# Transposes by DMA or by TensorE in a fused linear-attention and SwiGLU kernel

## The chip, the cores and the metric

The kernel runs on one core of a Trainium2 chip. The metric is the device time of one execution in microseconds (us). TensorE (PE) does the matrix products, VectorE (DVE), ScalarE (ACT) and GpSimd (POOL) the elementwise work, and SyncE (SP) and POOL issue the DMAs.

## The reference, cut to what matters

Eight batches of eight heads, 1024 tokens, head size 64. The keys and values are first projected along the sequence to 64 rows; the attention's output then runs through a gated feed-forward block (FFN) with 512 inputs and 1536 hidden units.

```python
k_proj = np.einsum('ks,bhsd->bhkd', E, k)          # (8, 8, 64, 64)
v_proj = np.einsum('ks,bhsd->bhkd', F, v)
scores = 1.0 / np.sqrt(64) * np.matmul(q, k_proj.transpose(0, 1, 3, 2))
attn = np.exp(scores - np.max(scores, axis=-1, keepdims=True))
attn = attn / (np.sum(attn, axis=-1, keepdims=True) + 1e-09)
x = np.matmul(attn, v_proj)                        # heads side by side: (8192, 512)
g = x @ w_gate
out = (g * (1.0 / (1.0 + np.exp(-g))) * (x @ w_val)) @ w_out
```

## The kernel before

The FFN is the frame. Its main loop has 192 iterations: 16 chunks of 512 tokens (two for each batch) by 12 blocks of 128 hidden units. An iteration has three groups of four matmuls with 512 columns each: `f_g` (gate, L303), `f_v` (value, L318) and, a chunk behind, `f_y` (output, L344). ScalarE takes a tanh of the gate (`th`, L311), VectorE makes the gated product in two instructions (L327, L332), and ScalarE copies the finished output block out of PSUM (`ysb`, L353) for SP to store.

The attention of the next batch is cut into small steps, and each is put by hand into a slot; every iteration has two slots, one after `f_g` and one after `f_y`. All engines run their instructions in the order in which this program writes them. The steps of batch b, for 8 units of work (`u`: 4 heads by 2 of the 8 token groups each):

- `u_KV`: k and v projected, 16 matmuls side by side (`kvp`, L150); v's result is written to the block diagonal of `BDV` (L164, L165).
- `u_KT`: the projected k transposed and put on the block diagonal of `BD` (L174, L182).
- `u_T`: four 128x128 transposes of q on TensorE into PSUM (`qTp`, L195) and a copy `qT` out of it. For batches 2 to 7 (`BY_DMA`) `u_TD` does this for half a batch with one DMA transpose from SP (`qTd`, L207).
- `u_S`: four score matmuls (`sc`, L229) and the exponential `ee` on ScalarE; `u_R`: sum and reciprocal on VectorE (`zz`, `rr`); `u_N`: the product on POOL (L260), which gives `AA`, or `AAd` for batches 2 to 7.
- `u_A`: four transposes of `AA` on TensorE (`aTp`, L276) and a copy `AT`. For batches 2 to 7 `u_AD` does this for half a batch with one DMA transpose from SP (L214).
- `u_PV`: one matmul for a pair of heads (`pv`, L287) and a copy into `xT`, the FFN's input.

`place(b)` gives the slots: a batch has 48 of them, and `s0 = 48 * (b - 1)` is where its projection stands. The loads of k, v and q (with a conversion to bf16) are issued from POOL, in POOL's order among its products. PSUM buffers for all attention steps in the loop come from one pool of three (`ps_a`).

Batch 0's first half comes ahead of the loop, in an order written out. k comes in four quarters by SP in float32 (`kraw`) and is converted head by head (`cast_k`), seven by VectorE and POOL and the last by ScalarE; POOL issues its loads of q, v and weights after its own conversion. `warm(n)` are n dummy matmuls whose results nothing reads.

Of the kernel before, what the change touches and what calls it, by code (L numbers as in the profile page):

```python
# [15 lines left out]
B = 8  # L16
H = 8
# [10 lines left out]
CH = 2  # L28
CW = 512
NIT = B * CH * NFT  # L30
BY_DMA = range(2, B)


@with_exitstack
def kernel(
# [22 lines left out]
    const = ctx.enter_context(tc.tile_pool(name="const", bufs=1))  # L58
    w_pool = ctx.enter_context(tc.tile_pool(name="weights", bufs=1))
    kv_pool = ctx.enter_context(tc.tile_pool(name="kv", bufs=2))  # L60
    q_pool = ctx.enter_context(tc.tile_pool(name="qbf", bufs=4))
    aw = ctx.enter_context(tc.tile_pool(name="aw", bufs=2))
    x_pool = ctx.enter_context(tc.tile_pool(name="xT", bufs=2))
# [76 lines left out]
    def u_KV(b, what="kv", hs=(0, H), at="a"):  # L140

        key = (b, what)
        if key not in kvp:
            kvp[key] = bank(at, [P, H, D], FP32, "kvp")
        t = kvp[key]
        h0, h1 = hs
        todo = [x for x in (("k", 0, ET, kb), ("v", 64, FT, vb)) if x[0] in what]
        for j in range(NJ):
            for _, lo, w, src in todo:
                nc.tensor.matmul(  # L150
                    out=t[lo : lo + 64, h0:h1].rearrange("p h d -> p (h d)"),
                    lhsT=w[:, j, :],
                    rhs=src[b][:, h0:h1, j, :],
                    start=(j == 0),
                    stop=(j == NJ - 1),
                )
        if "k" in what:
            if (b, "s") not in kvp:
                kvp[b, "s"] = aw.tile([KP, H, D], BF16, name="ks", tag="ks")
            nc.scalar.copy(out=kvp[b, "s"][:, h0:h1], in_=t[0:64, h0:h1])  # L160
        if "v" in what:
            tv = t[64:128].rearrange("p (a c) d -> p a c d", c=2)
            ps = slice(h0 // 2, h1 // 2)
            nc.vector.tensor_copy(out=BDV[b % 2][0:64, ps, 0:64], in_=tv[:, ps, 0, :])  # L164
            nc.vector.tensor_copy(out=BDV[b % 2][64:128, ps, 64:128], in_=tv[:, ps, 1, :])  # L165
        if h1 == H:
            kvp.pop(key)

# [32 lines left out]
        copy(eng, t[:], ps[:])  # L201
        qT[b, u] = t

    def u_TD(b, ch):

        t = aw.tile([P, 2 * H, P], BF16, name="qTd", tag="qTd")
        nc.sync.dma_start_transpose(  # L207
            out=t[:], in_=qb[b, ch][:].rearrange("p h j d -> p (h j d)")
        )
        qT[b, ch, "d"] = t  # L210

    def u_AD(b, ch):
        t = aw.tile([P, 4, NPAIR, P], BF16, name="AT", tag="AT")
        nc.sync.dma_start_transpose(  # L214
            out=t[:].rearrange("p j a t -> p (j a) t"),
            in_=AA.pop((b, ch, "d"))[:].rearrange("p j h k -> p (j h k)"),
        )
        AT[b, ch] = t

    def u_S(b, u, at="a"):  # L220
        ch, w = divmod(u, 4)
        g, i = divmod(w, 2)
        ps = bank(at, [P, 4, P], FP32, "sc")
        if b in BY_DMA:
            t = qT[b, ch, "d"][:].rearrange("p (h i) t -> p i h t", i=2)[:, i, 4 * g : 4 * g + 4]
        else:
            t = qT.pop((b, u))
        for n in range(4):
            nc.tensor.matmul(  # L229
                out=ps[:, n, :], lhsT=t[:, n, :], rhs=BD[b % 2][:, 4 * g + n, :], start=True, stop=True  # L230
            )
        e = aw.tile([P, 4, 2, KP], FP32, name="ee", tag="ee", bufs=4)
        nc.scalar.activation(  # L233
            out=e[:].rearrange("p h j k -> p (h j k)"),
            in_=ps[:].rearrange("p a k -> p (a k)"),
            func=AF.Exp,
            scale=scale,
        )
        ee[b, u] = e
# [7 lines left out]
        rr[b, u] = r  # L247

    def u_N(b, u):
        ch, w = divmod(u, 4)  # L250
        g, i = divmod(w, 2)
        if b in BY_DMA:
            if (b, ch, "d") not in AA:
                AA[b, ch, "d"] = aw.tile([P, 4, H, KP], BF16, name="AAd", tag="AAd")
            a = AA[b, ch, "d"][:, 2 * i : 2 * i + 2, 4 * g : 4 * g + 4, :]
        else:
            a = AA[b, u] = aw.tile([P, 2, 4, KP], BF16, name="AA", tag="AA", bufs=4)
            a = a[:]
        eng = nc.vector if b == 0 and u == 3 else nc.gpsimd
        eng.tensor_tensor(  # L260
            out=a.rearrange("p j h k -> p h j k"),
            in0=ee.pop((b, u))[:],
            in1=rr.pop((b, u))[:].unsqueeze(3).to_broadcast([P, 4, 2, KP]),
            op=ALU.mult,
        )

    def u_A(b, u, eng=nc.vector):
        ch, w = divmod(u, 4)
        g, i = divmod(w, 2)
        if (b, ch) not in AT:  # L270
            AT[b, ch] = aw.tile([P, 4, NPAIR, P], BF16, name="AT", tag="AT")
        ps = ps_a.tile([P, 2, 2, P], BF16, name="aTp", tag="pa")
        a = AA.pop((b, u))
        for pr in range(2):
            for j in range(2):
                nc.tensor.transpose(  # L276
                    out=ps[:, j, pr, :],
                    in_=a[:, j, 2 * pr : 2 * pr + 2, :].rearrange("p h k -> p (h k)"),
                    identity=ident_bf[:],
                )  # L280
        copy(eng, AT[b, ch][:, 2 * i : 2 * i + 2, 2 * g : 2 * g + 2, :], ps[:])

    def u_PV(b, ch, pr, eng=nc.scalar):
        if (b, ch) not in xT:
            xT[b, ch] = x_pool.tile([P, NPAIR, CW], BF16, name="xT", tag=f"xT{ch}")
        ps = ps_a.tile([P, CW], FP32, name="pv", tag="pa")
        nc.tensor.matmul(  # L287
            out=ps[:].rearrange("p (j t) -> p j t", t=P),
            lhsT=BDV[b % 2][:, pr, :],
            rhs=AT[b, ch][:, :, pr, :],  # L290
            start=True,
            stop=True,
        )
        copy(eng, xT[b, ch][:, pr, :], ps[:])
# [71 lines left out]
    def place(b):  # L366
        s0 = 48 * (b - 1)
        if b == 1:
            put(34, u_KV, 1, "k")
            put(36, u_KT, 1)  # L370
            put(41, u_KV, 1, "v")
            tt = (36, 37, 38, 39, 48, 50, 52, 54)
            sa = (37, 38, 39, 40, 49, 51, 53, 55)
            ta = (42, 43, 44, 45, 54, 56, 58, 60)
            sp = (45, 46, 46, 47, 62, 63, 64, 65)
        else:
            put(s0, u_KV, b)
            put(s0 + 3, u_KT, b)
            o = 14 if b == 2 else 6
            put(s0 + (3 if b == 2 else -6), u_TD, b, 0)  # L380
            put(s0 + (5 if b == 2 else -4), u_TD, b, 1)
            sa = [s0 + o + 3 * j for j in range(NJ)]
            put(sa[3] + 4, u_AD, b, 0)
            put(sa[7] + 4, u_AD, b, 1)
            sp = [s0 + i for i in (39, 41, 43, 45, 57, 59, 61, 63)]
        for j in range(NJ):
            if b not in BY_DMA:
                put(tt[j], u_T, b, j)
                put(ta[j], u_A, b, j)
            put(sa[j], u_S, b, j)  # L390
            put(sa[j] + 1, u_R, b, j)
            put(sa[j] + 1, u_N, b, j)
        for i in range(8):
            put(sp[i], u_PV, b, i // 4, i % 4)

# [4 lines left out]
    with tc.manual_schedule():  # L400
        ef = []
        for which, src in (("E", E), ("F", F)):
            raw = const.tile([KP, S], FP32, name=f"{which}raw")
            ef.append(raw)
        nc.sync.dma_start(out=ef[0][:], in_=E)
        kraw = [
            aw.tile([P, 2, NJ * D], FP32, name="kraw", tag=tag) for tag in ("qTd", "qTd", "AAd", "AAd")
        ]
        for i in range(4):
            nc.sync.dma_start(  # L410
                out=kraw[i][:],
                in_=k[0, 2 * i : 2 * i + 2].rearrange("h (p j) d -> p h (j d)", j=NJ),
            )
        nc.sync.dma_start(out=ef[1][:], in_=F)
# [6 lines left out]
        new_k(0)  # L421

        def cast_k(eng, h):
            copy(eng, kb[0][:, h].rearrange("p j d -> p (j d)"), kraw[h // 2][:, h % 2])

        def turn(which):
            for half in range(2):
# [21 lines left out]
        turn(0)  # L449
        warm(4)  # L450
        for h in range(7):
            cast_k(nc.gpsimd if h == 3 else nc.vector, h)
        load_q(0, 0, 2)
        load_v(0, 2)
        load_w_gv(0)
# [12 lines left out]
        u_S(0, 1, "g")  # L468
        u_S(0, 2, "a")
        u_S(0, 3, "a")  # L470
        for u in range(3):
            u_R(0, u)
            u_N(0, u)
        u_KV(0, "v", (0, 4), at="y")
        u_R(0, 3)
        u_N(0, 3)
        u_A(0, 0, nc.scalar)
        warm(2)
        u_A(0, 1, nc.scalar)
        u_KV(0, "v", (4, 8), at="y")  # L480
        u_A(0, 2, nc.scalar)
        u_PV(0, 0, 0, nc.vector)
        u_PV(0, 0, 1, nc.vector)
        u_A(0, 3, nc.scalar)
        u_PV(0, 0, 2, nc.scalar)
        u_PV(0, 0, 3, nc.vector)
        load_w_gv(2)
# [21 lines left out]
        for b in range(1, B):  # L509
            place(b)  # L510
        for b in range(2, B):
            s0 = 48 * (b - 1) - (12 if b == 2 else 24)
            put(s0, load_k, b)
            put(s0 + 2, load_v, b)
            put(s0 + 4, load_q, b, 0)
            put(s0 + 6, load_q, b, 1)

        for s in slots:
            slots[s].sort(key=lambda x: x[0] not in (load_k, load_v, load_q))
# [48 lines left out]
```

## Time and profile before

| | us |
|---|---|
| median of 3 runs (582.72 to 582.86) | 582.82 |
| the profiled execution | 582.86 |
| its span, first to last instruction | 581.1 |
| TensorE busy | 567.6 (98%) |
| VectorE busy | 337.7 (58%) |
| ScalarE busy | 242.4 (42%) |
| POOL busy | 106.8 (18%) |

The span is what the profile shows from the first instruction to the last; the profiled execution's own time has 1.8 us more around it. Busy times are sums of instruction lengths in which overlaps on an engine count once. A row of the timeline gives the start, the length, the engine, the line, the operation with its output and inputs, and in brackets how long the engine had been idle and what ended that. Matmuls are pipelined, so the pace of TensorE is read from one start to the next and not from a matmul's length.

### The profile page before, as it was taken

The numbers are of one execution on the slowest core, as the hardware profiler recorded it, in microseconds if no ns is written. First come the engines' busy times: TensorE is split into PE (matmuls) and PEld (weight loads), VectorE is DVE, ScalarE is ACT, GpSimd is POOL, SyncE is SP. The second block draws the span as 40 slices with busy tenths as digits, with TensorE's granted clock in tenths as the row PEclk, the third lists the DMA queues.
The fourth block names the chain that finished last, engine by engine and source line by source line (L and its number), as shares of the span: only waits on it lengthen the run. The fifth ranks groups of instructions, "written<-read, shape, count | busy, mean of one in ns | idle before, by whom it ended". The sixth has DMA issues, their size and how long they took to land.

```text
span 581.1 us, 7901 instructions
## 1 busy us (share of the span) xinstructions
PE 567.6 (98%) x2952; PEld 268.1 (46%) x2952; DVE 337.7 (58%) x576; ACT 242.4 (42%) x428; POOL 106.8 (18%) x119
## 2 busy tenths in 40 slices
PE   5999999999999999999999999999999999999997
PEld 3644444544444444444444444444444444444443
DVE  2787564766556664666546764566555674545550
ACT  2545435454435434354345434354343533443321
POOL 5625040224102320025001240022300220000000
PEclk9999999999999999999999999999999999999999
DMA  9999955309930399016980289313990124001012
GB/s 223 190 200 192 205 87 100 73 19 170 203 81 37 80 194 179 37 45 110 177 159 29 63 145 197 74 38 77 183 193 37 38 55 73 37 36 37 19 37 91
DMA packets 100599, 61.34 MB, mean 106 GB/s; under 512 B 51792, under 2 KB 91216, under 8 KB 100560
## 3 DMA queue, kind: packets, MB, share of 16 engines
q0 software_dynamic: 40176, 28.84, 34.3%
q1 hardware_dynamic: 60384, 31.99, 23.9%
q8 instruction: 23, 0.38, 0.3%
q14 instruction: 16, 0.13, 0.1%
HBM read 60.29 MB, written 16.78 MB: 133 GB/s over the span
## 4 chain that ended last, share of the span: by engine, by line
PE 94%; ACT 2%; DVE 2%; DMA 1%; issue 0%; SPq 0%; DVEq 0%; ACTq 0%
PE yps L344 28%; PE vps L318 28%; PE gps L303 28%; PE kvp L150 3%; PE sc L229 3%; PE pv L287 2%; DMA kraw<-in_k_dram 1%; DVE hT L332 1%; PE qTp L195 1%; PE aTp L276 1%; ACT qT L138 0%; DVE s L327 0%; DVE zz L244 0%; PE kTp L174 0%; ACT ysb L353 0%
## 5 line engine op out<-in xcount | busy, mean ns | idle before, releaser
L327 DVE SCALAR_TENSOR_TENSOR s<-th,gps 128x512 f32<-128x512 f32 x192 | 130.5, 680 | 136.1 <-ACT th L311 135.8
L303 PE MATMUL gps<-xT,wg 128*128 128x512 bf16 x768 | 197.9, 379 | 0.5 <-ACT xT L138 0.3
L318 PE MATMUL vps<-xT,wv 128*128 128x512 bf16 x768 | 197.2, 379 | 0.0
L344 PE MATMUL yps<-wo,hT 128*128 128x512 bf16 x768 | 194.6, 379 | 0.7 <-ACT ysb L353 0.7
L311 ACT ACTIVATE th<-gps 128x512 f32<-128x512 f32 x192 | 114.7, 597 | 154.4 <-PE gps L303 152.7
L332 DVE TENSOR_TENSOR hT<-s,vps 128x512 bf16<-128x512 f32 x192 | 132.0, 688 | 22.8 <-PE vps L318 2.5
L344 PEld LDWEIGHTS <-hT 128*128 128x128 bf16 x768 | 75.1, 98 | 91.5 <-issue 1.0
L318 PEld LDWEIGHTS <-wv 128*128 128x128 bf16 x768 | 72.9, 98 | 83.4 <-issue 4.0
L303 PEld LDWEIGHTS <-wg 128*128 128x128 bf16 x768 | 73.1, 98 | 81.9 <-issue 1.0
L260 POOL TENSOR_TENSOR AAd<-ee,rr 128x512 bf16<-128x512 f32 x48 | 49.9, 1040 | 300.6 <-issue 165.3
L353 ACT ACTIVATE ysb<-yps 128x512 f32<-128x512 f32 x64 | 38.2, 597 | 76.0 <-PE yps L344 76.0
L138 ACT CAST xT<-pv 128x512 bf16<-128x512 f32 x61 | 35.4, 584 | 50.4 <-PE pv L287 50.4
L244 DVE TENSOR_REDUCE zz<-ee 128x8 f32<-128x512 f32 x64 | 43.5, 680 | 20.0 <-ACT ee L233 19.7
L233 ACT ACTIVATE ee<-sc 128x512 f32<-128x512 f32 x64 | 38.0, 597 | 20.0 <-PE sc L229 18.8
L260 POOL TENSOR_TENSOR AA<-ee,rr 128x512 bf16<-128x512 f32 x15 | 15.5, 1040 | 63.7 <-DVE rr L246 25.8
L287 PE MATMUL pv<-AT,BDV 128*128 128x512 bf16 x64 | 23.6, 379 | 0.9 <-ACT AT L138 0.7
L229 PEld LDWEIGHTS <-qTd 128*128 128x128 bf16 x192 | 14.8, 98 | 11.3
L150 PE MATMUL kvp<-kb,ET 128*64 128x512 bf16 (+1 forms) x72 | 17.1, 389 | 1.7 <-POOL kb L138 1.0
L229 PE MATMUL sc<-BD,qTd 128*128 128x128 bf16 x192 | 18.6, 219 | 0.0
L246 DVE RECIPROCAL rr<-zz 128x8 f32<-128x8 f32 x64 | 13.0, 203 | 6.3
L164 DVE CAST BDV<-kvp 64x256 bf16<-64x256 f32 (+1 forms) x9 | 3.6, 396 | 22.3 <-ACT ks L160 20.0
L150 PE MATMUL kvp<-vb,FT 128*64 128x512 bf16 (+1 forms) x72 | 16.4, 375 | 0.0
(50 smaller groups left out, 157.1 us busy)
## 6 DMA issues: line engine op xcount, KB each, us to landing
out_dram<-ysb SPq DMA_DIRECT2D x64, 256.0 KB, 2.3
qb<-in_q_dram POOLq DMA_DIRECT2D x15, 512.0 KB, 17.2
kb<-in_k_dram POOLq DMA_DIRECT2D x7, 1024.0 KB, 11.5
vb<-in_v_dram POOLq DMA_DIRECT2D x7, 1024.0 KB, 14.0
kraw<-in_k_dram SPq DMA_DIRECT2D x4, 512.0 KB, 6.0
wg<-in_moe_w_gate_dram POOLq DMA_DIRECT2D x6, 256.0 KB, 10.2
wv<-in_moe_w_val_dram POOLq DMA_DIRECT2D x6, 256.0 KB, 10.7
wo<-in_moe_w_out_dram POOLq DMA_DIRECT2D x2, 768.0 KB, 15.4
```

The lines of the kernel that those rows point to most:

```text
L150: nc.tensor.matmul(out=t[lo : lo + 64, h0:h1].rearrange("p h d -> p (h d)"), lhsT=w[:, j, :], rhs=src[b][:, h0:h1, j, :], start=(j == 0), ...
L229: nc.tensor.matmul(out=ps[:, n, :], lhsT=t[:, n, :], rhs=BD[b % 2][:, 4 * g + n, :], start=True, stop=True)
L233: nc.scalar.activation(out=e[:].rearrange("p h j k -> p (h j k)"), in_=ps[:].rearrange("p a k -> p (a k)"), func=AF.Exp, scale=scale,)
L244: nc.vector.reduce_sum(out=z[:], in_=e[:], axis=AX.X)
L260: eng.tensor_tensor(out=a.rearrange("p j h k -> p h j k"), in0=ee.pop((b, u))[:], in1=rr.pop((b, u))[:].unsqueeze(3).to_broadcast([P, 4, 2 ...
L303: nc.tensor.matmul(out=ps[:], lhsT=wg[:, kt, f * P : (f + 1) * P], rhs=x[:, kt, :], start=(kt == 0), stop=(kt == NKT - 1),)
L311: nc.scalar.activation(out=th[:], in_=ps[:], func=AF.Tanh, scale=0.5)
L318: nc.tensor.matmul(out=ps[:], lhsT=wv[:, kt, f * P : (f + 1) * P], rhs=x[:, kt, :], start=(kt == 0), stop=(kt == NKT - 1),)
L327: nc.vector.scalar_tensor_tensor(out=s1[:], in0=th[:], scalar=1.0, in1=g[:], op0=ALU.add, op1=ALU.mult)
L332: nc.vector.tensor_tensor(out=hT[c][:, f, :], in0=s1[:], in1=ps[:], op=ALU.mult)
L344: nc.tensor.matmul(out=yy[c][:], lhsT=hT[c][:, f, i * P : (i + 1) * P], rhs=wo[:, f, :], start=(f == 0), stop=(f == NFT - 1),)
L353: nc.scalar.activation(out=ysb[:], in_=yy.pop(c)[:], func=AF.Copy, scale=0.5)
```

## The change

Batches 2 to 7 lose the DMA transposes: `u_TD`, `u_AD` and `BY_DMA` go, and all batches use `u_T` and `u_A`. `AT` is laid out with the pair of heads ahead of the token group, so that `u_PV` reads contiguous columns. The slots of batches 2 to 7 are new, and so are the slots of their loads. `kraw` gets a pool of its own in place of the buffers of `qTd` and `AAd`. In batch 0, POOL converts head 1 (in the first quarter of k) in place of head 3; ScalarE copies v's block diagonals; the sums and products of all four units stand ahead of v's projection, and the second half of v is projected after the fourth unit's transposes; some copies change between ScalarE and VectorE.

```diff
-BY_DMA = range(2, B)
...
+    raw_pool = ctx.enter_context(tc.tile_pool(name="raw", bufs=1))
...
-            nc.vector.tensor_copy(out=BDV[b % 2][0:64, ps, 0:64], in_=tv[:, ps, 0, :])
-            nc.vector.tensor_copy(out=BDV[b % 2][64:128, ps, 64:128], in_=tv[:, ps, 1, :])
+            eng = nc.vector if b else nc.scalar
+            copy(eng, BDV[b % 2][0:64, ps, 0:64], tv[:, ps, 0, :])
+            copy(eng, BDV[b % 2][64:128, ps, 64:128], tv[:, ps, 1, :])
...
-    def u_TD(b, ch):
-    def u_AD(b, ch):
...
-            AT[b, ch] = aw.tile([P, 4, NPAIR, P], BF16, name="AT", tag="AT")
+            AT[b, ch] = aw.tile([P, NPAIR, 4, P], BF16, name="AT", tag="AT")
...
-            rhs=AT[b, ch][:, :, pr, :],
+            rhs=AT[b, ch][:, pr].rearrange("p j t -> p (j t)"),
...
             put(s0, u_KV, b)
             put(s0 + 3, u_KT, b)
-            o = 14 if b == 2 else 6
-            put(s0 + (3 if b == 2 else -6), u_TD, b, 0)
-            put(s0 + (5 if b == 2 else -4), u_TD, b, 1)
-            sa = [s0 + o + 3 * j for j in range(NJ)]
-            put(sa[3] + 4, u_AD, b, 0)
-            put(sa[7] + 4, u_AD, b, 1)
-            sp = [s0 + i for i in (39, 41, 43, 45, 57, 59, 61, 63)]
+            tt = [s0 + 8 + 5 * j for j in range(NJ)]
+            sa = [t + 2 for t in tt]
+            ta = [t + 7 for t in tt]
+            sp = [s0 + i for i in (36, 39, 41, 44, 57, 59, 62, 64)]
         for j in range(NJ):
-            if b not in BY_DMA:
-                put(tt[j], u_T, b, j)
-                put(ta[j], u_A, b, j)
+            put(tt[j], u_T, b, j)
             put(sa[j], u_S, b, j)
             put(sa[j] + 1, u_R, b, j)
             put(sa[j] + 1, u_N, b, j)
+            put(ta[j], u_A, b, j)
...
-            cast_k(nc.gpsimd if h == 3 else nc.vector, h)
+            cast_k(nc.gpsimd if h == 1 else nc.vector, h)
...
-        for u in range(3):
+        for u in range(4):
             u_R(0, u)
             u_N(0, u)
+        warm(2)
+        u_A(0, 0, nc.scalar)
         u_KV(0, "v", (0, 4), at="y")
-        u_R(0, 3)
-        u_N(0, 3)
-        u_A(0, 0, nc.scalar)
-        warm(2)
         u_A(0, 1, nc.scalar)
+        u_A(0, 2, nc.scalar)
+        u_PV(0, 0, 0, nc.scalar)
+        u_PV(0, 0, 1, nc.vector)
+        u_A(0, 3, nc.vector)
         u_KV(0, "v", (4, 8), at="y")
-        u_A(0, 2, nc.scalar)
-        u_PV(0, 0, 0, nc.vector)
-        u_PV(0, 0, 1, nc.vector)
-        u_A(0, 3, nc.scalar)
         u_PV(0, 0, 2, nc.scalar)
         u_PV(0, 0, 3, nc.vector)
...
-            s0 = 48 * (b - 1) - (12 if b == 2 else 24)
-            put(s0, load_k, b)
-            put(s0 + 2, load_v, b)
-            put(s0 + 4, load_q, b, 0)
-            put(s0 + 6, load_q, b, 1)
+            s0 = 48 * (b - 2)
+            put(s0 + 36, load_k, b)
+            put(s0 + 40, load_v, b)
+            put(s0 + 36, load_q, b, 0)
+            put(s0 + 44, load_q, b, 1)
```

More of the change, by code (lines that the diff above doesn't have):

```diff
@@ L202, in u_T @@
         qT[b, u] = t
-    def u_TD(b, ch):
[L206 to L210, printed above, removed]
-    def u_AD(b, ch):
[L213 to L218, printed above, removed]
     def u_S(b, u, at="a"):
-        ch, w = divmod(u, 4)
-        g, i = divmod(w, 2)
+        g = (u % 4) // 2
         ps = bank(at, [P, 4, P], FP32, "sc")
[L224 to L227, printed above, removed]
+        t = qT.pop((b, u))
         for n in range(4):
@@ L249, in u_N @@
     def u_N(b, u):
[L250 to L258, printed above, removed]
+        a = aw.tile([P, 2, 4, KP], BF16, name="AA", tag="AA", bufs=4)
         eng = nc.vector if b == 0 and u == 3 else nc.gpsimd
         eng.tensor_tensor(
-            out=a.rearrange("p j h k -> p h j k"),
+            out=a[:].rearrange("p j h k -> p h j k"),
             in0=ee.pop((b, u))[:],
@@ L265, in u_N @@
         )
+        AA[b, u] = a
     def u_A(b, u, eng=nc.vector):
@@ L276, in u_A @@
                 nc.tensor.transpose(
-                    out=ps[:, j, pr, :],
+                    out=ps[:, pr, j, :],
                     in_=a[:, j, 2 * pr : 2 * pr + 2, :].rearrange("p h k -> p (h k)"),
@@ L280, in u_A @@
                 )
-        copy(eng, AT[b, ch][:, 2 * i : 2 * i + 2, 2 * g : 2 * g + 2, :], ps[:])
+        copy(eng, AT[b, ch][:, 2 * g : 2 * g + 2, 2 * i : 2 * i + 2, :], ps[:])
     def u_PV(b, ch, pr, eng=nc.scalar):
@@ L287, in u_PV @@
         nc.tensor.matmul(
-            out=ps[:].rearrange("p (j t) -> p j t", t=P),
+            out=ps[:],
             lhsT=BDV[b % 2][:, pr, :],
-            rhs=AT[b, ch][:, :, pr, :],
+            rhs=AT[b, ch][:, pr].rearrange("p j t -> p (j t)"),
             start=True,
@@ L405 @@
         nc.sync.dma_start(out=ef[0][:], in_=E)
-        kraw = [
-            aw.tile([P, 2, NJ * D], FP32, name="kraw", tag=tag) for tag in ("qTd", "qTd", "AAd", "AAd")
-        ]
+        kraw = raw_pool.tile([P, H, NJ * D], FP32, name="kraw")
         for i in range(4):
             nc.sync.dma_start(
-                out=kraw[i][:],
+                out=kraw[:, 2 * i : 2 * i + 2],
                 in_=k[0, 2 * i : 2 * i + 2].rearrange("h (p j) d -> p h (j d)", j=NJ),
@@ L423, in cast_k @@
         def cast_k(eng, h):
-            copy(eng, kb[0][:, h].rearrange("p j d -> p (j d)"), kraw[h // 2][:, h % 2])
+            copy(eng, kb[0][:, h].rearrange("p j d -> p (j d)"), kraw[:, h])
         def turn(which):
```

## Prediction

> **What bounds the kernel now.** I read the page first, then TensorE's list of waits, then the windows, and last the timeline around the operations that the change moves. The page's span, busy times and chain of waits:
>
> ```profile
> span 581.1 us, 7901 instructions
> PE 567.6 (98%) x2952; PEld 268.1 (46%) x2952; DVE 337.7 (58%) x576; ACT 242.4 (42%) x428; POOL 106.8 (18%) x119
> PE 94%; ACT 2%; DVE 2%; DMA 1%; issue 0%; SPq 0%; DVEq 0%; ACTq 0%
> ```
>
> TensorE is busy for 98% of the span and holds 94% of the chain; VectorE and ScalarE are about half idle. A busy TensorE need not be one at its peak, so I ask what it waits for. All its waits of the whole run, with total, times, longest (us):
>
> ```profile
> PE efp L431 <- DMA Eraw<-in_E_dram: 4.6, 1, 4.6
> PE kvp L150 <- POOL kb L138: 1.0, 1, 1.0
> PE kvp L150 <- ACT kb L138: 0.7, 1, 0.7
> PE yps L344 <- ACT ysb L353: 0.7, 1, 0.7
> PE pv L287 <- ACT AT L138: 0.7, 1, 0.7
> ```
>
> The longest are all in the first 26 us, but for the 0.7 us on ysb, which is in the tail. The same list for 120 to 565 us alone is empty. Two answers show that this middle is also dense: one stretch of the windows, and the chain's pieces for the k and v projections of batches 3 and 4 (start, length).
>
> ```profile
> 300.00:365.00 65.00, 65.00 (x336) 30.41 (x336) 39.18 (x66) 27.62 (x49) 11.87 (x12) 1.00 0.61 107
> ```
>
> ```profile
> 164.18 1.85 PE kvp L150 x16
> ...
> 232.13 1.85 PE kvp L150 x16
> ```
>
> One batch period is 232.13 - 164.18 = 67.95 us. It holds 24 FFN iterations of three groups of four 512-column matmuls; a group takes 0.864 us from its start to the next start in the timeline, so 72 x 0.864 = 62.2. With the projections (1.85), eight groups of scores (8 x 0.22), eight PV matmuls (8 x 0.215) and the four small transposes of k (0.22), that is 67.75. So 0.2 us of the period is slack: there is no gap into which TensorE work could be put for nothing.
>
> **Part 1, the transposes of batches 2 to 7.** Removed: 24 DMA transposes on SP's queue (12 of q, 12 of the normalised scores). Added for each of 6 batches and 8 units: four 128x128 transposes of q and a copy qT on ScalarE, four 128x128 transposes of AA and a copy AT on VectorE. Counting the two instruction lists gives 6 x 8 x 2 = 96 groups of four on TensorE, 384 transposes, each with its weight load; 48 more qT copies on ScalarE and 48 more AT copies on VectorE. All other counts in the middle stay.
>
> What does a group cost? Batches 0 and 1 do exactly this already, so the trace has the row (start, length, then what; the next start is what counts, since lengths overlap):
>
> ```profile
> 84.48 0.39 PE L276 MATMUL aTp<-ident_bf,AA 128*128 128x128 bf16 x4
> 84.71 1.03 PE L303 MATMUL gps<-xT,wg 128*128 128x512 bf16 x4
> 85.57 0.39 PE L276 MATMUL aTp<-ident_bf,AA 128*128 128x128 bf16 x4
> 85.80 1.03 PE L318 MATMUL vps<-xT,wv 128*128 128x512 bf16 x4
> ```
>
> 84.71 - 84.48 = 0.23 us for four, and the group behind it again takes its usual 0.86 (84.71 to 85.57). The groups at 81.67 and 98.37 give 0.22 and 0.23. A second bound comes from a period that holds such work: from batch 2's projections (93.77) to batch 3's (164.18) is 70.41, 2.46 more than the later periods, for eight transpose groups and four score groups more: 0.205 each. So 0.205 to 0.23; I take 0.22, the nearest to most rows: 96 x 0.22 = **+21.1 us** (19.7 to 22.1), all on the path, because TensorE has no idle time there. As a share of the middle: 3.5 us on each of six periods.
>
> The Trainium skill ("TensorE: Matmul & The Clock Gate", Part 4) speaks against this edit more strongly: about 275 ns for a transpose in a kernel, and transposes that do not count as activity for the clock gate. By that figure the sum would be 384 x 0.275 = 106 us; the 84.48 row has about 57 ns for each, and the stretch from 70 to 160 us, which holds such groups, a granted clock of 1.00, so I use the rows. The same page's sustained spacing for 128 columns with weight loads (section "Back-to-back issue gap", 81 ns) would make it 31 us; no row after 30 us shows that pace.
>
> The copies: 48 x 0.58 = 28 us on ScalarE (L138 qT, 580 ns) and 48 x 0.42 = 20 us on VectorE (AT, 424 ns). They are hidden: in the 65 us stretch above ScalarE has 37 us free and VectorE 26, and a period adds 4.6 and 3.4 us. What would uncover them is a short distance. For batch 0 the scores come one slot after the transpose and wait: the group at 38.60 (q) is followed by vps at 38.83, and the scores start at 39.93 instead of 39.69, 0.24 late. The new slots put scores two slots after q's transpose (about 2.9 us) and AA's transpose four slots after the normalisation; on average a copy has twice the room. I put this at 0, with 48 x 0.24 = 11.5 us if the cover is gone (rival 3).
>
> Removing the DMA transposes frees SP's queue, where outputs stand behind them, and DMA time. Nothing on TensorE waits for either from 120 to 565 us, so the gain is 0. PV's moving operand becomes contiguous: a pv matmul in the strided form is already spaced 0.21 us (87.75 to 87.96), the pace of any 512 columns, so 0.
>
> The loads of batch b move later: k and the first q to 12 slots ahead of the projection (24 before), v to 8. By POOL's order, which runs a DMA issue when the normalisation before it has ended, v is issued behind the normalisation of slot 12 ahead. Twelve slots are six iterations of 3 x 0.864 and about 2.1 us of small groups, 17.6; that normalisation ends some 2.8 us into them (116.7 to 119.8 from scores to normalisation, less a slot's 1.3, plus its 1.04): 14.8 us are left. In the trace v lands 13.2 to 14.9 us after issue, with q and transposes beside it; with the transposes gone and k issued 7 us rather than 3.6 us earlier I expect under 12. So 0, with rival 2 if not.
>
> **Part 2, the start.** The first FFN matmul is at 25.36 us and the last copy that its first group needs ends at 26.25. The rows (start, length, engine):
>
> ```profile
> 7.66 0.86 POOL L138 CAST kb<-kraw 128x512 bf16<-128x512 f32 x1 [5.84 <-DMA kraw<-in_k_dram]
> 8.47 1.79 POOL L110 DMA_DIRECT2D qb<-in_q_dram  x2
> ...
> 11.47 0.62 ACT L138 CAST kb<-kraw 128x512 bf16<-128x512 f32 x1 [0.63 <-DMA kraw<-in_k_dram]
> ...
> 24.93 0.59 PE L287 MATMUL pv<-AT,BDV 128*128 128x512 bf16 x2 [0.67 <-ACT AT L138]
> ...
> 25.56 0.69 DVE L138 CAST xT<-pv 128x512 bf16<-128x512 f32 x1 [0.56 <-PE pv L287]
> ```
>
> (a) POOL now casts head 1, which lands with the first quarter at 5.70, so q's load is issued at 5.70 + 0.86 = 6.56 instead of 8.47, 1.9 us earlier; v's and the first weights' issues follow it. But q is not late today: its transposes follow kTp without a wait. And k is still moving: its quarters land at 5.70, 7.63, 8.98 and 11.47, and the last, which shares the engines with q from about 9 us, took 2.5 us instead of 1.4 to 1.9. The earlier q shares with two quarters. TensorE's second half of k waits for that landing. So no gain, and 0 to +1.9; I take +0.6, nearer to the 0.6 to 1.1 us that today's sharing costs one quarter.
>
> (b) The new order for batch 0: all four reduces go ahead of v's projection, two dummy matmuls fill in, then AA's transposes, with v's second half behind the fourth. The third unit's reduce no longer stands behind v's diagonals on VectorE (VectorE waited 0.29 us there, normalisation 3 ended at 23.16). ScalarE in exchange gets four diagonal copies (about 0.3 us each by VectorE's 0.29 for 64x128) in its queue, and PV of pairs 2 and 3 now waits for v's second half and its copies. Re-timing the rows: AA 0 is ready at 20.2 in both; v's first half ends at 21.6 at full pace or 22.5 at the pace of 18.93 (1.92 us for eight); ScalarE then has two diagonals (0.6), AT 1, AT 2 and xT 0 (0.58 each) in line; AA 3's transpose follows, v's second half, two more diagonals, PV, and the last xT at 26.8 or 27.7 against 26.25: +0.6 to +1.5. From below, the two waits of TensorE just ahead of the first FFN group (0.24 and 0.67) are all that can be saved: -0.9. I take +0.4.
>
> Behind this the FFN runs on as before, so the start adds **+1.0 us** (-0.9 to +3.4). The warm clock is the unsure piece: 512-column matmuls run at 0.46 us until 7.5 and at 0.22 from 21, though the granted clock reads 1.00.
>
> **Sum.** The profiled execution took 582.86 us, its span 581.1 and 1.8 around it; the median is 582.82, the same within 0.04. 582.86 + 21.1 + 1.0 = **605.0 us**. Its own range: 582.9 + 19.7 - 0.9 = 601.7 to 582.9 + 22.1 + 3.4 = 608.4.
>
> **Rivals.** 1, not slower: the transposes slip beneath the long matmuls, as TensorE's busy time is modelled. It decides if a group costs under 0.012 us (1.2 us, 0.2%, over 96), giving 582 to 584; the rows above have 0.22 for every group, so 2%. 2, v comes late: if a landing takes 16 us instead of under 14.8, each of five projections (batches 3 to 7) waits 1.2 us or more, +6 and up: 611 to 616. Against it, less traffic beside it; 6%. 3, the scores wait for the qT copies as in batch 0: +11.5, 616; against it, the double distance; 5%. 4, TensorE stays at half pace longer in the start, because it now waits for AA 0 and does less before: each us at half pace loses 0.5, +3 to +5 beyond my value: 608 to 610; 9%.
>
> **How the numbers follow.** My forecast has 78%. The range 602.3 to 608.5 takes nearly all of it and part of rival 4; rivals 1 to 3 are left out, with a little of the low end. About 0.2%, 1.2 us, is what a measurement of this kernel can tell from no change: faster 0.01, same 0.01 (both rival 1), slower 0.98.
>
> **What would show it.** Right: periods of batches 3 to 7 of 71.3 to 71.6 us instead of 67.95, 256 transposes each of q and AA at 0.22 us for four, still no waits of TensorE in the middle, the first FFN group up to 2 us later. Wrong: a period under 70 (a group is cheaper), waits of kvp on a landing (rival 2), of sc on qT (rival 3), or half-pace matmuls past 23 us (rival 4).

## The result, and the profile after

| | before | changed |
|---|---|---|
| median (4 runs each) | 582.84 us | 605.09 us |
| lowest to highest | 582.72 to 583.03 | 603.61 to 606.30 |
| ratio to before, 95% interval | | 1.038 (1.0354 to 1.0406) |
| profiled execution, its span | 582.86, 581.1 | 604.41, 602.6 |

The forecast was 605.0 us, in a range from 602.3 to 608.5. The page of the changed kernel, with the same lines as before:

```profile
span 602.6 us, 8703 instructions
...
PE 587.3 (97%) x3336; PEld 287.4 (48%) x3336; DVE 356.5 (59%) x620; ACT 266.8 (44%) x480; POOL 106.9 (18%) x119
...
PE 93%; ACT 2%; DVE 2%; DMA 1%; issue 0%; SPq 0%; POOL 0%; DVEq 0%; ACTq 0%
```

TensorE has 384 instructions more (3336 - 2952), which are the 384 transposes, and 19.7 us more busy time. It holds the chain as it did. VectorE's 18.8 and ScalarE's 24.4 us of added copies leave both far from full. TensorE's waits between 120 and 590 us, with total, times and longest, are one line:

```profile
PE yps L318 <- ACT ysb L327: 0.7, 1, 0.7
```

It is the same 0.7 us of the tail as before. So no new wait came into the middle, and the added time there is work. The chain's pieces for the projections of batches 3 and 4:

```profile
167.33 1.85 PE kvp L150 x16
...
238.86 1.85 PE kvp L150 x16
```

A period is 238.86 - 167.33 = 71.53 us, against 67.95: 3.58 more, inside the 71.3 to 71.6 that was forecast. TensorE's timeline shows why (start, length):

```profile
197.78 0.39 PE L250 MATMUL aTp<-ident_bf,AA 128*128 128x128 bf16 x4
198.00 0.39 PE L210 MATMUL sc<-BD,qT 128*128 128x128 bf16 x4
198.22 1.03 PE L292 MATMUL vps<-xT,wv 128*128 128x512 bf16 x4
```

Four transposes take 0.22 us from their start to the next start, exactly as the four score matmuls behind them.

The profile also splits the whole run. Before, batch 2's projections start at 93.77 us and 487.3 us remain to the end of the span; in the changed kernel they start at 93.57 and 509.0 remain. The middle and tail therefore cost 21.7 us. The start came out 0.2 us earlier in this one execution, but the runs of one kernel now spread by 2.7 us, so the start needs more than one profile.

### The profile page after: what moved, and what is told of

Read it like the earlier page. It is cut to its first block, busy times and chain, and to the rows that moved or that the text cites. A ratio compares the mean times of both kernels' runs of the same rounds, so it can differ in the third digit from the quotient of the medians.

```text
span 602.6 us, 8703 instructions
## 1 busy us (share of the span) xinstructions
PE 587.3 (97%) x3336; PEld 287.4 (48%) x3336; DVE 356.5 (59%) x620; ACT 266.8 (44%) x480; POOL 106.9 (18%) x119
## 4 chain that ended last, share of the span: by engine, by line
PE 93%; ACT 2%; DVE 2%; DMA 1%; issue 0%; SPq 0%; POOL 0%; DVEq 0%; ACTq 0%
PE yps L318 27%; PE vps L292 27%; PE gps L277 27%; PE kvp L150 3%; PE sc L210 2%; PE pv L261 2%; PE aTp L250 2%; PE qTp L196 2%; DMA kraw<-in_k_dram 1%; DVE hT L306 1%; ACT ee L214 0%; ACT qT L138 0%; DVE s L301 0%; DVE zz L225 0%; ACT ysb L327 0%
## 5 line engine op out<-in xcount | busy, mean ns | idle before, releaser
L233 POOL TENSOR_TENSOR AA<-ee,rr 128x512 bf16<-128x512 f32 x63 | 65.5, 1041 | 411.7 <-DVE rr L227 271.8
L327 ACT ACTIVATE ysb<-yps 128x512 f32<-128x512 f32 x64 | 38.2, 597 | 71.3 <-PE yps L318 71.3
L138 ACT COPY qT<-qTp 128x512 bf16<-128x512 bf16 x62 | 36.0, 582 | 24.8 <-PE qTp L196 24.8
L138 DVE COPY AT<-aTp 128x512 bf16<-128x512 bf16 x61 | 25.7, 422 | 22.4 <-PE aTp L250 21.7
L250 PEld LDWEIGHTS <-AA 128*128 128x128 bf16 x256 | 19.3, 98 | 17.5 <-POOL AA L233 3.1
L250 PE MATMUL aTp<-ident_bf,AA 128*128 128x128 bf16 x256 | 24.8, 219 | 1.9 <-POOL AA L233 1.6
L210 PE MATMUL sc<-BD,qT 128*128 128x128 bf16 x256 | 24.8, 219 | 1.4 <-ACT qT L138 0.6
L196 PEld LDWEIGHTS <-qb 128*128 128x128 bf16 x256 | 19.0, 98 | 12.6 <-issue 0.6
L196 PE MATMUL qTp<-ident_bf,qb 128*128 128x128 bf16 x256 | 24.4, 219 | 0.0
```

What stands on the lines that cost most here:

```text
L138: (nc.scalar.copy if eng is nc.scalar else eng.tensor_copy)(out=out, in_=in_)
L196: nc.tensor.transpose(out=ps[:, n, :], in_=src[:, 4 * g + n, 2 * i : 2 * i + 2, :].rearrange("p j d -> p (j d)"), identity=ident_bf[:],)
L233: eng.tensor_tensor(out=a[:].rearrange("p j h k -> p h j k"), in0=ee.pop((b, u))[:], in1=rr.pop((b, u))[:].unsqueeze(3).to_broadcast([P, 4 ...
L250: nc.tensor.transpose(out=ps[:, pr, j, :], in_=a[:, j, 2 * pr : 2 * pr + 2, :].rearrange("p h k -> p (h k)"), identity=ident_bf[:],)
L327: nc.scalar.activation(out=ysb[:], in_=yy.pop(c)[:], func=AF.Copy, scale=0.5)
```

## The experiments

Theory A: the change costs TensorE's time for 96 groups of transposes, and the rest is small. The rivals were that waits, copies or the DMA transposes hold a part, or the start. Times are compared with the kernel before in the same series of runs, where its median lay between 581.6 and 582.2 us.

### The new start alone

The kernel before, with the changed kernel's start.

```diff
-            cast_k(nc.gpsimd if h == 3 else nc.vector, h)
+            cast_k(nc.gpsimd if h == 1 else nc.vector, h)
...
+            eng = nc.vector if b else nc.scalar
+            copy(eng, BDV[b % 2][0:64, ps, 0:64], tv[:, ps, 0, :])
+            copy(eng, BDV[b % 2][64:128, ps, 64:128], tv[:, ps, 1, :])
...
+        for u in range(4):
+            u_R(0, u)
+            u_N(0, u)
+        warm(2)
...
```

> The kernel before with the new start alone (POOL converts head 1, ScalarE copies batch 0's diagonals, new order of batch 0); the DMA transposes and all slots stay. Theory A (the transposes carry all the cost, the start saves a little): the profile of the changed kernel has its first FFN group at 24.75 us instead of 25.36, so 582.2, within 0.6 us of the kernel before. Theory B (the start costs what was forecast): 583.3 to 584.5. Second question, the spread of the changed kernel (603.6 to 606.3 over four runs, against 582.7 to 583.0): if it comes from the start, these runs spread by 2 us or more; if from the middle, by under 0.5 us.

It took 583.48 us against 581.97, a ratio of 1.0024 (1.0012 to 1.0036): 1.4 us slower (0.7 to 2.1). Theory A had the sign of the start wrong, having read it from one profile. The spread could not be told apart by this series: both kernels spread by over 2 us (12 runs 582.2 to 584.9, 17 runs of before 581.0 to 583.9), so it is not the change's own.

The profile places 0.8 to 1.1 of the 1.4 us. From the start of the scores of batch 0's units 1 to 3 to the first FFN group it takes 25.36 - 17.10 = 8.26 us in the new order. The kernel before has 25.36 - 17.51 = 7.85, with its scores at half pace, and the two kernels with the old order under "The new middle alone" and "Term (a) alone" have 7.63 and 7.58: 0.4 to 0.7 us. The first FFN group to batch 2's projections takes 68.82 us against 68.41, 0.41 more, through one wait that all profiles of the new order have and none of the old one. TensorE's timeline of this kernel:

```profile
17.10 1.00 PE L230 MATMUL sc<-BD,qT 128*128 128x128 bf16 x12
...
24.91 0.61 PE L288 MATMUL pv<-AT,BDV 128*128 128x512 bf16 x2 [0.63 <-ACT BDV L138]
25.36 1.32 PE L304 MATMUL gps<-xT,wg 128*128 128x512 bf16 x4
...
49.69 0.40 PE L277 MATMUL aTp<-ident_bf,AA 128*128 128x128 bf16 x4 [0.37 <-POOL AA L261]
```

The same stretch of the kernel before:

```profile
17.51 1.49 PE L229 MATMUL sc<-BD,qT 128*128 128x128 bf16 x12
...
25.36 1.32 PE L303 MATMUL gps<-xT,wg 128*128 128x512 bf16 x4
```

The first wait is that of PV on ScalarE's copies of v's second half to the diagonal. Before, the same matmuls waited 0.67 us on AT: one wait has been replaced by another of nearly the same length, and the path to it is longer. The second wait is on POOL's product for the last unit of batch 0. That product is late, and so is all of VectorE's work from the reciprocal of the second unit in the loop on, which starts at 44.88 us instead of 44.46; what that reciprocal waits for was not found.

### The new middle alone

The changed kernel with the old start.

```diff
-            cast_k(nc.gpsimd if h == 1 else nc.vector, h)
+            cast_k(nc.gpsimd if h == 3 else nc.vector, h)
...
-            eng = nc.vector if b else nc.scalar
...
-        for u in range(4):
+        for u in range(3):
             u_R(0, u)
             u_N(0, u)
...
```

> The changed kernel with the old start (POOL converts head 3, VectorE copies the diagonals, old order of batch 0); the transposes of batches 2 to 7 on TensorE, the new slots and loads stay. Theory A: 96 groups of 0.224 us = 21.5 us on 582.8, 604.3, periods of 71.53 us, first FFN group back at 25.4. Theory B (part of the cost is the start's): 602.5 to 603.8. The spread: if it comes from the new start, these runs stay within 0.5 us; if from the middle, they spread by 2 us.

603.93 us, ratio 1.0373 (1.0353 to 1.0394): 21.7 us on 582.0. From batch 2's projections (93.09) to the end of the span (602.2) are 509.1 us, as in the changed kernel, and 21.8 more than before: 0.226 to 0.227 a group. Theory A holds for the middle.

### q's load let go by the second quarter again

```diff
-            cast_k(nc.gpsimd if h == 1 else nc.vector, h)
+            cast_k(nc.gpsimd if h == 3 else nc.vector, h)
```

This is in the changed kernel.

> The changed kernel, with POOL converting head 3 again, so that q's first load is let go after k's second quarter. The forecast's term (a) had the earlier release cost 0 to 1.9 us through k's landing: then k's last quarter lands earlier here than the 10.85 us of the changed kernel, and the time is 0.6 us lower, 604.5. The rival (release is free or helps, since k landed at 10.85 there against 11.47 in the kernel before): k's last quarter lands at 11.4 to 11.5, TensorE's second half of k starts 0.6 us later, and the time is 0.3 to 0.6 us higher, 605.5.

605.21 us, ratio 1.0398 (1.0379 to 1.0418), which overlaps the changed kernel's interval. k's last quarter was converted from 12.1 us on, later than in the changed kernel (10.85) or the kernel before (11.47), against the forecast's term (a), but a landing of one execution proves little. From the scores to the first FFN group it took 8.31 us, though TensorE ran the scores at half pace (the row of twelve score matmuls is 1.49 us long, against 1.01 in the changed kernel).

### Term (a) alone

The kernel before with head 1 on POOL, and nothing else.

> The kernel before with one edit: POOL converts head 1, so q's first load is let go by k's first quarter; batch 0's order stays. With the whole new start the kernel before was 1.4 us slower (ratio 1.0012 to 1.0036). If term (a) of the forecast (the earlier q load delays k) is behind that: +0.6 to +1.4 us. If it is the new order (b): no change, within 0.5 us.

581.67 us, ratio 0.9999 (0.9987 to 1.0011). The earlier release of q does nothing that shows, so term (a) is 0 within 0.8 us, and the start's 1.4 us belongs to the order and the diagonals.

### The transposes of q twice

In batches 2 to 7 of the changed kernel each transpose of q is issued twice into the same place.

```diff
-        for n in range(4):
+        for n in [n for n in range(4) for _ in range(2 if b > 1 else 1)]:
             nc.tensor.transpose(
```

> The changed kernel with every transpose of q in batches 2 to 7 issued twice into the same PSUM place: 48 more groups of four on TensorE, with no further copy, DMA or wait. Theory A (the cost of the change is TensorE's own time, 0.224 us a group): 48 x 0.224 = 10.8 us more than the changed kernel, about 616, period 71.53 + 1.79 = 73.3 us. Theory B (a good part of the 21.6 us is for copies, waits and distances that come with a transpose): clearly less, under 6 us.

614.06 us, ratio 1.0559 (1.0536 to 1.0583), 0.0179 above the changed kernel's: 10.4 us. The pieces of its chain:

```profile
241.61 1.85 PE kvp L150 x16
...
314.92 1.85 PE kvp L150 x16
```

The period is 73.31, 1.78 us more for 8 groups, 0.223 each. These transposes came with no copy, wait or DMA, so a group's price is TensorE's own time. It comes to 56 ns for a transpose from one start to the next, where the Trainium skill ("TensorE: Matmul & The Clock Gate", Part 4) has about 275 ns in a kernel; the measurement decides. The page's figure is one transpose's duration, which is 219 ns in the changed kernel's rows; what the time pays for is the spacing.

### The DMA transposes put back, idle

The changed kernel with 24 DMA transposes of q from SP whose results nothing reads.

```diff
+    def u_XD(b, ch):
+        t = aw.tile([P, 2 * H, P], BF16, name="xd", tag="xd", bufs=1)
+        nc.sync.dma_start_transpose(
+            out=t[:], in_=qb[b, ch][:].rearrange("p h j d -> p (h j d)")
+        )
...
+            for i, d in enumerate((4, 18, 32, 40)):
+                put(s0 + d, u_XD, b, i % 2)
```

> The changed kernel with 24 DMA transposes of q issued again from SP in batches 2 to 7, into a buffer that nothing reads (as many as the change removed, between the stores of the output). Theory A (nothing on TensorE's path waits for them, so taking them away gained nothing): 605, within 1 us of the changed kernel, periods of 71.53 us. Theory B (their removal gained time, which the added transposes hid in the sum): slower by 1 us or more, periods above 71.6.

609.72 us, ratio 1.0473 (1.0449 to 1.0498): (1.0473 - 1.038) x 582 = 5.4 us above the changed kernel, which I had not expected. The list of waits names the cause:

```profile
PE kvp L150 <- DMA vb<-in_v_dram: 2.5, 3, 1.1
```

For batches 3 to 7 v's load took 15.8 to 17.1 us to land instead of 12.3 to 13.3, and the new slots leave 167.26 - 151.59 = 15.7 us between its issue and its use. This is the forecast's rival 2, which the changed kernel misses by 2.4 us. The list's 2.5 us count only the time in which TensorE had nothing running. From the FFN group ahead of the projections to the one behind them these five batches take 3.8 us more than in the changed kernel, which covers all of this profile's longer middle (512.6 us against 509.0); its start was 1.1 us later as well. Does anything else cost? The same kernel with the loads of batches 3 to 7 twelve slots earlier:

```diff
+            e = 0 if b == 2 else 12
-            put(s0 + 36, load_k, b)
+            put(s0 + 36 - e, load_k, b)
...
```

> The kernel with 24 idle DMA transposes, with the loads of k, v and q for batches 3 to 7 put 12 slots earlier. Theory A (the idle transposes cost time only by making v land late: v took 15.8 to 17.1 us, and 15.7 us are left between its issue and its use): with 12 slots more there is no wait of kvp on vb, periods are 71.53 us, 604 to 605.5. Theory B (the transposes cost time in another way as well, on TensorE or on the stores): 607 or more, periods above 71.6.

604.66 us, ratio 1.0391 (1.0373 to 1.0409), no wait on v, periods of 71.53 us (238.83 to 310.36). So the DMA transposes cost TensorE's periods nothing but through the landing, and taking them away gained nothing by itself, within the 2 us or so that the two intervals leave open.

### Scores one slot behind q's transpose

```diff
-            sa = [t + 2 for t in tt]
+            sa = [t + 1 for t in tt]
```

> The changed kernel with the scores of batches 2 to 7 one slot behind q's transpose instead of two. Theory A (the copies on ScalarE are hidden by the distance of two slots; at one slot each group of scores is about 0.24 us late, as in batch 0): 48 x 0.24 = 11.5 us more at most, 610 to 617, with waits of sc on qT in the list. Theory B (ScalarE has room at any distance): no change, 605.

624.76 us, ratio 1.0764 (1.0723 to 1.0804), 22 us above the changed kernel, and not for the reason that either theory gave. The list has no wait of the scores of batches 2 to 7 on qT; v's load is late. The waits of TensorE, and POOL's timeline of this kernel:

```profile
PE kvp L150 <- DMA vb<-in_v_dram: 11.5, 5, 3.1
```

```profile
151.35 0.94 POOL L90 DMA_DIRECT2D kb<-in_k_dram  x1
152.29 0.88 POOL L110 DMA_DIRECT2D qb<-in_q_dram  x1
153.15 0.89 POOL L100 DMA_DIRECT2D vb<-in_v_dram  x1
```

The same rows of the changed kernel:

```profile
144.88 0.94 POOL L90 DMA_DIRECT2D kb<-in_k_dram  x1
145.82 0.88 POOL L110 DMA_DIRECT2D qb<-in_q_dram  x1
...
151.59 0.94 POOL L100 DMA_DIRECT2D vb<-in_v_dram  x1
```

Moving the scores moved the normalisations by one slot, and one of them now stands ahead of k's load in POOL's program. k, q and v are issued together, 6.5 us later for k, and v lands 16.4 to 17.7 us after its issue. Nothing in the edit touches a load.

The 11.5 us of waits are not all that it cost: the middle of this profile takes 527.2 us against 509.0. From the FFN group ahead of the projections to the one behind them the five batches take 15.9 us more than in the changed kernel. Part of that is pace: in batches 4 and 5, after waits of 2.5 and 2.3 us, the granted clock is 0.50 to 0.51 from 245 to 248 us and from 320 to 323, and the matmuls run at half pace. With the loads twelve slots earlier:

> The kernel with scores one slot behind q's transpose, with the loads for batches 3 to 7 put 12 slots earlier. Theory A (what it lost was v's landing alone: moved one slot, the normalisation stands ahead of the load of k in POOL's order, so k, q and v are issued together and v lands 16.4 to 17.7 us later): no wait of kvp, 604 to 605.5; the qT copies are hidden at one slot too. Theory B (the short distance costs time as well): above 607, with waits of sc on qT.

607.81 us, ratio 1.0438 (1.0423 to 1.0452), about 3 us above the changed kernel, and between the theories. v lands in time, in 10.8 to 11.6 us, and no wait of kvp is left. The period is 71.78 us, 0.25 more: one group of scores a period, at 206.29, starts 0.24 us late. Its rows, and those of a group that is on time:

```profile
204.96 0.39 PE L196 MATMUL qTp<-ident_bf,qb 128*128 128x128 bf16 x4
205.19 1.03 PE L277 MATMUL gps<-xT,wg 128*128 128x512 bf16 x4
206.29 0.40 PE L210 MATMUL sc<-BD,qT 128*128 128x128 bf16 x4
...
219.51 0.39 PE L196 MATMUL qTp<-ident_bf,qb 128*128 128x128 bf16 x4
219.73 1.03 PE L277 MATMUL gps<-xT,wg 128*128 128x512 bf16 x4
220.59 0.39 PE L210 MATMUL sc<-BD,qT 128*128 128x128 bf16 x4
```

In both only one FFN group lies between the transposes and the scores. In the late one ScalarE runs the output copy `ysb` first (from 205.16), so the qT copy starts 0.70 us behind the transposes' start; in the other it starts 0.42 us behind. Six late groups are 1.5 us. The profiled start was also 2.2 us later (batch 2's projections at 95.74), and one profile cannot say whether that is the slots.

### More transposes by DMA

If a group costs 0.226 us and a DMA transpose nothing, the way on is the other one: the kernel before with part of batch 1 moved to DMA too. First both halves of q and the second half of the scores:

```diff
-BY_DMA = range(2, B)
+Q_DMA = {(b, ch) for b in range(1, B) for ch in range(2)}
+A_DMA = Q_DMA - {(1, 0)}
...
+            put(34, u_TD, 1, 0)
+            put(38, u_TD, 1, 1)
+            put(58, u_AD, 1, 1)
```

> The kernel before with batch 1 moved to DMA transposes too: both halves of q and the second half of the normalised scores, 12 groups of four less on TensorE; batch 1's slots are moved a little for that. Theory A (a group costs 0.226 us on TensorE's path and a DMA transpose nothing while its result is in time): 12 x 0.226 = 2.7 us less than the kernel before, 579 to 580. Rival (the transposes stand in SP's queue ahead of the stores, or compete with the loads of batch 2, and TensorE waits): same or slower than before, with waits of sc, pv or kvp in 60 to 130 us.

584.40 us, ratio 1.0035 (1.0016 to 1.0053): slower, the rival's way. TensorE's waits after the start have one new line:

```profile
PE sc L230 <- DMA qTd<-qb: 4.2, 1, 4.2
```

The first half's transpose landed only at 73.6 us, in the stretch in which weights, k, q and v all arrive. The wait cost more than its 4.2 us: the granted clock is 0.50 from 75 to 78 us, and eight FFN matmuls there take 3.27 us from start to start instead of 1.72. With that half left on TensorE:

```diff
-Q_DMA = {(b, ch) for b in range(1, B) for ch in range(2)}
-A_DMA = Q_DMA - {(1, 0)}
+A_DMA = {(b, ch) for b in range(1, B) for ch in range(2)} - {(1, 0)}
...
-            put(34, u_TD, 1, 0)
-            put(38, u_TD, 1, 1)
+            put(40, u_TD, 1, 1)
```

> The kernel before with only the second half of batch 1 moved to DMA transposes, q and scores: 8 groups of four less on TensorE. Theory A (the kernel with the first half's q by DMA lost 4.2 us at 73 us waiting for one DMA transpose among the loads, and the rest of its saving was real): no wait of sc on qTd, 8 x 0.226 = 1.8 us less than the kernel before, ratio about 0.997, and 68.6 us from batch 2's projections to batch 3's instead of 70.41. Rival (fewer groups do not shorten the time): 582, ratio 1.000.

580.59 us, ratio 0.9968 (0.9956 to 0.9979): 1.9 us faster than the kernel before, 1.2 to 2.6 by the interval, and the fastest kernel of this study. Its chain:

```profile
93.82 1.85 PE kvp L150 x16
...
162.67 1.85 PE kvp L150 x16
```

From batch 2's projections to batch 3's it takes 68.85 us, against 70.41, and to the end of the span 485.6 against 487.3: 1.75 us for 8 groups, 0.22 each.

## Why the prediction was right

**The reading of what bounds the kernel** held: with no slack in a period, the added TensorE work came out as added time, and the forecast's period of 71.3 to 71.6 us was measured as 71.53. That 605.0 meets 605.09 so closely is luck: the middle came out 0.6 us above its forecast, the start 0.4 above its own, and the interval of the ratio is 1.5 us to either side.

**The price of a group** was taken as 0.22 us, 21.1 us for 96. It is 0.226 by the remaining time (21.7 us), and 0.223 by doubling q's transposes. The lower bound of 0.205, from the difference of two periods, was too low. The 106 us that the prediction set against it multiplies a duration and not a spacing.

**The copies** are hidden, as forecast. The 0.24 us wait (rival 3) does not come with one slot's distance as such: at one slot it came once in eight groups, where one FFN group alone lies between and ScalarE has an output copy to run first.

**The removed DMA transposes** were worth nothing on TensorE's path by themselves. But they and the later loads belong together. The forecast had v landing in under 12 us with 14.8 us to spare; it took 12.3 to 13.3 of 15.7. Rival 2, which was priced at 6 us and more, stayed away by 2.4 us; with the DMA transposes back it cost 5.4 us, and 19 when POOL's order shifted (a ratio of 1.0764 against 1.0438 with the loads early).

**The start** was forecast at +1.0 us and measured at +1.4 (0.7 to 2.1), with its two terms wrong in opposite directions. The step that failed is (a): the earlier q load was to delay k by 0.6 us, and alone it changes nothing (0.9999). Term (b), the new order, was given +0.4, between a bound of -0.9 and a re-timing of +0.6 to +1.5; the re-timing was near (0.4 to 0.7 up to the first FFN group), and 0.41 came later in the loop, where the forecast said the FFN runs on as before.

**Rival 4**, half pace in the start, was wrong in its price. The profile of the changed kernel was at full pace from 14.65 us and the one with POOL's head 3 at half pace until 18.4, yet from the scores to the first FFN group they take 8.27 and 8.31 us: the first wait on POOL's product is 1.27 us long in the one and 0.80 in the other, and absorbs the difference.

## What to carry to other kernels

When the busiest engine's list of waits is empty and a period's work adds up to its length, as here, an instruction moved onto that engine costs its spacing, and one moved off it gains as much, if what replaces it lands in time. Price it by start-to-start rows of the same instruction in the same kernel. Before moving a step, write down which DMA issues stand behind it in its engine's program and how many microseconds lie between each landing and its first use: a slot's shift of the scores cost 22 us, mostly through a load that the edit did not name.

## What the runs showed of the hardware that was not expected

The same kernel's runs spread by 0.3 us in the first series (582.72 to 583.03) and by 3 us in later ones (580.75 to 584.08 in one). In the profiles of kernels that share their middle and tail, batch 2's projections start at different times (93.09 to 94.27 us in three that do the changed kernel's middle, with 509.0 to 509.1 us left in each), so what varies between these profiles is the start. Six profiles of kernels that are the same up to batch 2's projections reach them between 92.75 and 95.74 us. TensorE's full pace in the start began at 14.65 us in one execution and at about 21 in another, with a granted clock of 1.00 in both profiles; the changed kernel with POOL's head 3 showed 0.53 from 15 to 18 us while its score matmuls ran at the same half pace.

A wait in a dense stretch can cost more than its length. After waits of 2.5, 2.3 and 4.2 us (scores one slot behind, more transposes by DMA) the granted clock was 0.50 to 0.51 for about 3 us. After waits of 1.8, 1.9 and 3.1 us in the first of these kernels it stayed at 1.00, so the length of the wait alone does not decide, and what does stays open.
